# Block-sparse attention with a gated FFN: the first batch's k and q in fp32 on the hardware DMA queue, v loaded directly beside its ones column, weights held back, filler matmuls at the head

## The chip, the cores and the metric

The kernel runs on one core of one Trainium2 chip. The metric is the device time of one execution in microseconds (us). The kernel before took 298.56 us (median; 298.49 to 298.87). A profile gives the span from the first to the last instruction, which is just under 2 us shorter than the device time of the same run. The profiled run is a run of its own: that of the kernel before took 299.34 us.

Engine names follow the profile: PE is the matmul engine, PEld its weight load, DVE the vector engine, ACT the scalar engine, POOL the GpSimd engine, SP the engine that issues part of the DMAs. "L272" is line 272 of the kernel in question, so the same statement has different numbers in different kernels.

## The reference, cut to what matters

```python
def _attn_ref(q, k, v, sampled_blocks):          # q, k, v: (4, 8, 768, 64) fp32
    scores = scale * np.matmul(q, k.transpose(0, 1, 3, 2))
    mask = ...   # blocks of 32: neighbours, first and last row and column, 3 sampled blocks
    scores = np.where(mask, scores, -1000000000.0)
    scores = scores - np.max(scores, axis=-1, keepdims=True)
    attn = np.exp(scores)
    attn = attn / (np.sum(attn, axis=-1, keepdims=True) + 1e-09)
    return np.matmul(attn, v)

def _moe_ref(x, w_gate, w_val, w_out):           # x: (3072, 512), from the attention's output
    gate = 1.0 / (1.0 + np.exp(-(x @ w_gate)))
    val = x @ w_val                              # 512 -> 1536
    return gate * val @ w_out                    # 1536 -> 512
```

## The kernel before: the parts that the change touches

The work is split into 12 units: 4 batches, and 3 query ranges of 256 tokens in each. A unit has 4 head pairs. The row sum of the softmax comes free: the tile `vex` holds v in columns 0 to 63 of every row and a constant 1.0 in column 64, so the product with the exponentials gives the sum as its 65th column. A small scheduler (`plan`) fixes, in Python, the order in which every engine gets its instructions. On the chip each engine then works through its list in that order.

Loads:

```python
    k16 = sing.tile([128, H, NT, D], f16)
    v16 = sing.tile([128, H, NT, D], f16)
    vex = [sing.tile([128, H, NT, D + 1], f16, name=f"vex{r}") for r in range(2)]
    # ... cut ...
    def load_heads(dst, src, b, h0, h1, t0=0, t1=NT):
        nc.gpsimd.dma_start(                       # fp32 in DRAM, cast to f16 by the DMA
            dst[:, h0:h1, t0:t1, :],
            src[b, h0:h1].rearrange("h (p t) d -> p h t d", t=NT)[:, :, t0:t1, :],
        )
    # ... cut ...
    nc.sync.dma_start(e64, e64_h.ap())
    nc.scalar.dma_start(sbi, sampled_blocks)
    nc.sync.dma_start(mc, mc_h.ap())
    nc.sync.dma_start(ident, ident_h.ap())
    for p in range(NP):
        load_heads(k16, k, 0, 2 * p, 2 * p + 2)
        load_heads(q16, q, 0, 2 * p, 2 * p + 2, 0, 2)      # only unit 0's part of q
        load_heads(v16, v, 0, 2 * p, 2 * p + 2)
    load_w(0)
    load_heads(q16, q, 0, 0, H, 2, NT)                     # the rest of q: units 1 and 2
    for j in range(1, NF // FCH):
        load_w(j)
    # ... cut ...
    nc.vector.memset(mb16, 0.0)
    junk = sing.tile([128, 512], f16)
    nc.vector.memset(junk, 0.0)
    for r in range(2):
        nc.vector.memset(vex[r][:, :, :, D : D + 1], 1.0)  # the ones column
```

The head of the program: the block mask is made on DVE, one matmul with the constant `e` spreads it into `bias`, and v is copied into `vex` by DVE:

```python
    def mask_blocks(eng):
        sbf = sing.tile([NB, 3], f32, name="sbf")
        nc.vector.tensor_copy(sbf, sbi.bitcast(u16)[:, 0:12:4])
        nc.vector.tensor_tensor(mc[:, :, 1:4], ...)        # cut: is_equal
        # ... cut: tensor_reduce into mb16 ...

    warm(6)                                                # 6 matmuls on zeros
    t_mb = plan.add([(DVE, 0.7)], mask_blocks, at=2.5)
    # ... cut ...
    mm = plan.add([(PE, 0.25)], bias_mm, [t_mb], take=[bank])        # reads e and mb16
    plan.add([(PE, 0.9)], lambda eng: warm(2), [mm])

    def vcopy(b, p, deps, at):
        def go(eng):
            nc.vector.tensor_copy(
                vex[b % 2][:, 2 * p : 2 * p + 2, :, 0:D],
                v16[:, 2 * p : 2 * p + 2, :, :],
            )
        # ... cut ...
```

Each pair's k and q go through a DVE copy (`pr`), PE transposes, and a copy into `kT` and `qT`. From batch 1 on, DMA transposes issued by SP do this instead. Batch 1's own loads, all with `load_heads`, are:

```python
            def load(eng):
                for dst, src in ((k16, k), (q16, q), (v16, v)):
                    load_heads(dst, src, 1, 0, H)
```

The softmax here doesn't subtract the row's maximum and nothing guards it: scores larger than these inputs give would overflow.

## Time and profile before

| | kernel before |
|---|---|
| device time, median (range) | 298.56 us (298.49 to 298.87) |
| span of the profiled run | 297.6 us |
| PE busy | 289.9 us, 97% |
| first q·k matmul of unit 0 / 1 / 2 / 3 | 7.61 / 25.45 / 42.81 / 65.67 us |
| every later unit | 22.64 us after the one before |

Profile page of the kernel before: busy us, share of the span and instructions; then the busy share of PE, and the granted clock, in 40 equal slices as tenths (9 is 90% or more); then the chain of waits by engine.

```profile
PE 289.9 (97%) x3302; PEld 206.2 (69%) x3302; DVE 191.0 (64%) x439; ACT 205.1 (69%) x323; POOL 48.5 (16%) x65
...
PE   7998999999999999999999999999999999999994
...
PEclk9999999999999999999999999999999999999999
...
PE 92%; ACT 2%; DMA 2%; DVE 1%; POOL 1%; issue 0%; ACTq 0%; POOLq 0%
```

PE is full in every slice but the first ones. A change of the loads can only win in the head.

Timeline of PE in the kernel before: start, duration, engine, line, operation, output and input; in brackets the idle time before it and what ended it.

```profile
4.19 0.60 PE L300 MATMUL m<-e,mb 24*128 24x512 f16 x1 [0.20 <-DVE mb L252]
...
9.64 1.03 PE L382 MATMUL m<-ident,pr 128*128 128x128 f16 x8 [0.37 <-DVE pr L373]
10.61 0.39 PE L451 MATMUL s<-bias,e 64*128 64x256 f16 x2
10.80 0.42 PE L459 MATMUL s<-qT,kT 64*128 64x256 f16 x2
...
14.27 0.27 PE L459 MATMUL s<-qT,kT 64*128 64x256 f16 x2
14.38 0.27 PE L451 MATMUL s<-bias,e 64*128 64x256 f16 x2
...
15.46 0.61 PE L382 MATMUL m<-ident,pr 128*128 128x128 f16 x8
```

The same eight transposes take 1.03 us at 9.64 and 0.61 us at 15.46: PE runs at half rate at first. The page's clock row says 9 throughout and does not show this. The trace's clock records fit it: there is none before 13.30 us, and that one says full rate.

The chain of waits of the kernel before, in order of time: start, duration, what.

```profile
2.78 0.70 POOL v L188
3.48 5.72 DMA k<-in_k_dram
9.20 0.02 issue
9.23 0.37 DVE pr L373
9.60 0.05 issue
9.64 1.03 PE m L382 x8
```

The second pair's k holds PE until 9.64 us. This wait and the half rate are what the change aims at.

### The profile page before, as it was taken

The page shows a single profiled execution, that of the slowest core. Times are in us where ns is not written, and L with a number is a line of the kernel's source. Part 1 is how long each engine was busy: PE and PEld are TensorE (multiplying, and loading weights), DVE is VectorE, ACT ScalarE, POOL GpSimd, SP SyncE. Part 2 cuts the span into 40 slices and gives each one's busy share as a digit, 9 for nine tenths or more (in the row PEclk, how much of TensorE's full clock was granted, in tenths as well). Part 3 has the DMA queues.
Part 4 walks back from the last instruction along what each step waited for, and adds up shares of the span by engine and source line. Part 5 has one row for each costly group of instructions (what it writes and reads, how often), then busy time and mean ns, then how long its engine had stood idle before and what let it go on. Part 6 is the DMA issues. An engine that isn't in the chain of part 4 may idle for free.

```text
span 297.6 us, 7862 instructions
## 1 busy us (share of the span) xinstructions
PE 289.9 (97%) x3302; PEld 206.2 (69%) x3302; DVE 191.0 (64%) x439; ACT 205.1 (69%) x323; POOL 48.5 (16%) x65
## 2 busy tenths in 40 slices
PE   7998999999999999999999999999999999999994
PEld 2655785786786786786776786686687687687771
DVE  3588877875675677676576577577477477475240
ACT  2689977677677677677777776777777677672331
POOL 8944100197000000097100000000000000000000
PEclk9999999999999999999999999999999999999999
DMA  7999999999900200999940202920201200201101
GB/s 109 185 201 203 206 204 205 212 174 149 193 12 9 90 13 10 173 177 133 179 70 18 83 11 56 203 64 20 79 11 20 79 11 20 78 15 20 70 2 71
DMA packets 74540, 28.55 MB, mean 96 GB/s; under 512 B 57352, under 2 KB 71560, under 8 KB 74504
## 3 DMA queue, kind: packets, MB, share of 16 engines
q0 software_dynamic: 40400, 14.16, 43.7%
q1 hardware_dynamic: 33924, 13.75, 20.5%
q8 instruction: 26, 0.43, 0.6%
q10 hardware_dynamic: 180, 0.13, 0.1%
q14 instruction: 10, 0.08, 0.1%
HBM read 28.55 MB, written 6.29 MB: 117 GB/s over the span
## 4 chain that ended last, share of the span: by engine, by line
PE 92%; ACT 2%; DMA 2%; DVE 1%; POOL 1%; issue 0%; ACTq 0%; POOLq 0%
PE m L617 44%; PE m L657 22%; PE s L459 12%; PE m L497 12%; DMA k<-in_k_dram 2%; ACT pt L469 2%; PE s L451 1%; PE m L382 1%; PE m L347 1%; ACT qT L232 0%; PE m L518 0%; POOL k L188 0%; ACT kT L232 0%; POOL q L188 0%; POOL v L188 0%
## 5 line engine op out<-in xcount | busy, mean ns | idle before, releaser
L469 ACT ACTIVATE pt<-s 128x1024 f16<-128x1024 f32 x144 | 139.9, 1023 | 9.5 <-PE s L459 9.4
L475 DVE TENSOR_TENSOR pt<-pt,mask 128x1024 f16<-128x1024 f16 x132 | 91.0, 690 | 52.0 <-ACT pt L469 51.9
L628 ACT ACTIVATE th<-m 128x256 f32<-128x256 f32 x144 | 54.3, 388 | 48.0 <-PE m L617 47.2
L617 PE MATMUL m<-xT,wg 128*128 128x256 f16 x576 | 86.8, 273 | 0.3 <-DVE x L509 0.3
L617 PE MATMUL m<-xT,wv 128*128 128x256 f16 x576 | 86.4, 273 | 0.0
L633 DVE SCALAR_TENSOR_TENSOR ht<-th,m 128x256 f16<-128x256 f32 x144 | 56.6, 417 | 20.8 <-ACT th L628 20.5
L657 PE MATMUL m<-wo,ht 128*128 128x512 f16 x288 | 66.1, 380 | 0.0
L617 PEld LDWEIGHTS <-wv 128*128 128x128 f16 x576 | 56.3, 98 | 6.5
L617 PEld LDWEIGHTS <-wg 128*128 128x128 f16 x576 | 50.5, 98 | 14.8 <-issue 9.7
L657 PEld LDWEIGHTS <-ht 128*128 128x128 f16 x288 | 26.5, 98 | 32.8 <-issue 4.2
L459 PE MATMUL s<-qT,kT 64*128 64x256 f16 x576 | 48.0, 275 | 1.1 <-ACT pt L469 0.8
L497 PEld LDWEIGHTS <-pt 128*128 128x128 f16 x1152 | 43.3, 98 | 3.8 <-issue 0.6
L497 PE MATMUL m<-vex,pt 128*128 128x65 f16 x1152 | 45.1, 194 | 0.0
L459 PEld LDWEIGHTS <-kT 64*128 64x128 f16 x576 | 23.0, 95 | 17.4 <-issue 13.6
L694 ACT ACTIVATE ysb<-m 128x512 f32<-128x512 f32 x23 | 13.7, 597 | 23.7 <-PE m L657 23.7
L740 POOL DMA_DIRECT2D kp<-in_k_dram x16 | 13.0, 820 | 80.8 <-DMA kT<-kp 53.7
L509 DVE TENSOR_TENSOR x<-m,rz 128x256 f16<-128x256 f32 x48 | 20.4, 424 | 1.7
L507 DVE RECIPROCAL rz<-m 128x4 f32<-128x4 f32 x48 | 8.7, 181 | 15.1 <-PE m L497 15.1
L740 POOL DMA_DIRECT2D qp<-in_q_dram x16 | 13.0, 819 | 2.2 <-DMA kp<-in_k_dram 1.9
L451 PE MATMUL s<-bias,e 64*128 64x256 f16 x48 | 7.2, 319 | 0.2 <-ACT pt L469 0.2
L382 PE MATMUL m<-ident,pr 128*128 128x128 f16 x48 | 5.2, 264 | 0.8 <-DVE pr L373 0.4
L234 DVE CAST mask<-m 128x512 f16<-128x512 f32 x9 | 5.7, 681 | 0.4 <-PE m L347 0.4
(45 smaller groups left out, 67.2 us busy)
## 6 DMA issues: line engine op xcount, KB each, us to landing
out_dram<-ysb SPq DMA_DIRECT2D x23, 256.0 KB, 2.0
v<-in_v_dram POOLq DMA_DIRECT2D x3, 768.0 KB, 11.1
wg<-in_moe_w_gate_dram POOLq DMA_DIRECT2D x4, 384.0 KB, 12.8
wv<-in_moe_w_val_dram POOLq DMA_DIRECT2D x4, 384.0 KB, 14.0
wo<-in_moe_w_out_dram POOLq DMA_DIRECT2D x3, 512.0 KB, 16.9
kp<-in_k_dram POOLq DMA_DIRECT2D x16, 96.0 KB, 5.8
qp<-in_q_dram POOLq DMA_DIRECT2D x16, 96.0 KB, 4.9
k<-in_k_dram POOLq DMA_DIRECT2D x4, 192.0 KB, 5.8
```

The lines of the kernel that those rows point to most:

```text
L451: nc.tensor.matmul(score[self.bank.slot][:, o // D, i, :], e64[o : o + D, t * 128 : (t + 1) * 128], bias[o : o + D, :], start=True, stop=F ...
L459: nc.tensor.matmul(score[self.bank.slot][:, o // D, i, :], kT[b % 2][o : o + D, p, t * 128 : (t + 1) * 128], qT[b % 2][o : o + D, p, u * U ...
L469: nc.scalar.activation(self.pt, score[self.bank.slot], AF.Exp, bias=0.0, scale=SCALE)
L475: nc.vector.tensor_tensor(self.pt, self.pt, m.unsqueeze(1).broadcast_to([128, 2, 2, UQ]), op=ALU.mult,)
L497: nc.tensor.matmul(self.acc[:, s, a, :], self.steps[t // 2].pt[:, a, t % 2, s * 128 : (s + 1) * 128], vex[self.b % 2][:, 2 * self.p + a, t ...
L509: nc.vector.tensor_tensor(self.x16, self.acc[:, :, :, 0:D], rz.broadcast_to([128, 2, 2, D]), op=ALU.mult,)
L617: nc.tensor.matmul(pg[:, i, :], w[:, c, f * 128 : (f + 1) * 128], xTs[self.n][0][:, c, :], start=(c == 0), stop=(c == 3),)
L628: nc.scalar.activation(th, spare[bank.slot][:, 0:UQ], AF.Tanh, bias=0.0, scale=0.5)
L633: nc.vector.scalar_tensor_tensor(self.ht[:, f, :], in0=box[0], scalar=1.0, in1=spare[bank.slot][:, UQ : 2 * UQ], op0=ALU.add, op1=ALU.mult,)
L657: nc.tensor.matmul(spare[bank.slot], self.ht[:, f, s * 128 : (s + 1) * 128], wo[:, f, :], start=(f == 0), stop=(f == NF - 1),)
L694: nc.scalar.activation(ysb, spare[bank.slot], AF.Copy, bias=0.0, scale=0.5)
L740: nc.gpsimd.dma_start(dst[:, p, :, a, :], src[b, 2 * p + a].rearrange("(n t) d -> n t d", t=NT),)
```

## The change

The intent has four parts.

- The first batch's k and q come in fp32 through the SP queue. The DVE copies, which exist anyway, cast them.
- v is cast by its load and lands directly in columns 0 to 63 of `vex`, one DMA per head. The 16 DVE copies of v fall away, in all batches.
- The rest of q and the weights are held back until the second pair's k has been copied.
- 14 small matmuls on zeros fill PE's early gaps, so that the clock is released sooner.

```diff
+    k32 = (twice...)                    # cut: k of batch 0 in fp32 shares its tile with k16 and kp
+    q32 = sing.tile([128, H, UQ // 128, D], f32)
-    v16 = sing.tile([128, H, NT, D], f16)
+    def load_values(b, h0, h1):
+        for h in range(h0, h1):
+            load_heads(vex[b % 2][:, :, :, 0:D], v, b, h, h + 1)
-    nc.sync.dma_start(e64, e64_h.ap())
     nc.scalar.dma_start(sbi, sampled_blocks)
-    nc.sync.dma_start(mc, mc_h.ap())
-    nc.sync.dma_start(ident, ident_h.ap())
+    nc.scalar.dma_start(mc, mc_h.ap())
     for p in range(NP):
-        load_heads(k16, k, 0, 2 * p, 2 * p + 2)
-        load_heads(q16, q, 0, 2 * p, 2 * p + 2, 0, 2)
-        load_heads(v16, v, 0, 2 * p, 2 * p + 2)
-    load_w(0)
-    load_heads(q16, q, 0, 0, H, 2, NT)
-    # cut: the other weights
+        load_heads(k32, k, 0, 2 * p, 2 * p + 2, eng=nc.sync)
+        load_heads(q32, q, 0, 2 * p, 2 * p + 2, 0, 2, eng=nc.sync)
+        if p == 0:
+            nc.sync.dma_start(ident, ident_h.ap())
+            nc.sync.dma_start(e64, e64_h.ap())
+        load_values(0, 2 * p, 2 * p + 2)
+    def load_rest(gate):                 # called at the second pair's copy of k
+        first = load_heads(q16, q, 0, 0, H, 2, NT)
+        tc.add_manual_dep(first.ins, gate.name, ...)          # cut
+        # cut: all weights
@@ the ones column stays where it was, now after these loads in the program @@
     for r in range(2):
         nc.vector.memset(vex[r][:, :, :, D : D + 1], 1.0)
@@
+    for _ in range(FILL):                # FILL = 14
+        filler()                         # a 128x256 matmul on zeros, when nothing else is ready
-    plan.add([(PE, 0.9)], lambda eng: warm(2), [mm])
-    # cut: vcopy and its calls
@@ batch 1 @@
-                for dst, src in ((k16, k), (q16, q), (v16, v)):
+                for dst, src in ((k16, k), (q16, q)):
                     load_heads(dst, src, 1, 0, H)
+                load_values(1, 0, H)
@@ cut: batches 2 and 3 load v with load_values too; costs and landing times in the scheduler @@
```

More of the change, by code (lines that the diff above doesn't have):

```diff
@@ L37 @@
 FFN_LAG = 3
+GATE = 1
+FILL = 14
 TOK = (np.arange(S) % 128) * NT + np.arange(S) // 128
@@ L64, in __init__, with add @@
         self.tasks = []
+        self.rank = []
         self.room = {kind: [(0.0, i) for i in range(n)] for kind, n in banks.items()}
-    def add(self, engines, fn, deps=(), at=0.0, take=(), free=(), lag=None):
+    def add(self, engines, fn, deps=(), at=0.0, take=(), free=(), lag=None, late=0):
         self.tasks.append((engines, fn, list(deps), at, list(take), list(free), lag))
+        self.rank.append(len(self.tasks) - 1 + late)
         return len(self.tasks) - 1
@@ L77, in run @@
                 after[d].append(i)
-        ready = sorted(i for i in range(n) if not left[i])
+        ready = sorted((i for i in range(n) if not left[i]), key=self.rank.__getitem__)
         busy = {PE: 0.0, ACT: 0.0, DVE: 0.0, DMA: 0.0}
@@ L90, in run @@
                     if not left[j]:
-                        bisect.insort(ready, j)
+                        bisect.insort(ready, j, key=self.rank.__getitem__)
             if events and events[0][0] <= now:
@@ L177 @@
     q16 = sing.tile([128, H, NT, D], f16)
-    k16 = sing.tile([128, H, NT, D], f16)
     qp = sing.tile([128, NP, NT, 2, D], f16, name="qp")
-    kp = sing.tile([128, NP, NT, 2, D], f16, name="kp")
-    v16 = sing.tile([128, H, NT, D], f16)
+    twice = sing.tile([128, 2, H * NT * D], f16, name="twice")
+    k16 = twice[:, 0, :].rearrange("a (h t d) -> a h t d", h=H, t=NT)
+    kp = twice[:, 1, :].rearrange("a (p t h d) -> a p t h d", p=NP, t=NT, h=2)
+    k32 = (
+        twice.rearrange("a r n -> a (r n)")
+        .bitcast(f32)
+        .rearrange("a (h t d) -> a h t d", h=H, t=NT)
+    )
+    q32 = sing.tile([128, H, UQ // 128, D], f32)
     vex = [sing.tile([128, H, NT, D + 1], f16, name=f"vex{r}") for r in range(2)]
@@ L184, with load_heads @@
     kT = [sing.tile([128, NP, S], f16, name=f"kT{r}") for r in range(2)]
-    def load_heads(dst, src, b, h0, h1, t0=0, t1=NT):
-        nc.gpsimd.dma_start(
+    def load_heads(dst, src, b, h0, h1, t0=0, t1=NT, eng=None):
+        return (eng or nc.gpsimd).dma_start(
             dst[:, h0:h1, t0:t1, :],
@@ L196, in load_w @@
         f0, f1 = j * FCH * 128, (j + 1) * FCH * 128
-        for dst, src in ((wg, moe_w_gate), (wv, moe_w_val)):
+        return [
             nc.gpsimd.dma_start(
@@ L200, in load_w @@
             )
+            for dst, src in ((wg, moe_w_gate), (wv, moe_w_val))
+        ][0]
     def load_wo(j):
@@ L209 @@
     sbi = sing.tile([NB, 3], mybir.dt.int64)
-    nc.sync.dma_start(e64, e64_h.ap())
     nc.scalar.dma_start(sbi, sampled_blocks)
-    nc.sync.dma_start(mc, mc_h.ap())
-    nc.sync.dma_start(ident, ident_h.ap())
+    nc.scalar.dma_start(mc, mc_h.ap())
     for p in range(NP):
-        load_heads(k16, k, 0, 2 * p, 2 * p + 2)
-        load_heads(q16, q, 0, 2 * p, 2 * p + 2, 0, 2)
-        load_heads(v16, v, 0, 2 * p, 2 * p + 2)
-    load_w(0)
-    load_heads(q16, q, 0, 0, H, 2, NT)
-    for j in range(1, NF // FCH):
-        load_w(j)
-    for j in range(3):
-        load_wo(j)
+        load_heads(k32, k, 0, 2 * p, 2 * p + 2, eng=nc.sync)
[6 more added lines that the diff above has]
+        first = load_heads(q16, q, 0, 0, H, 2, NT)
+        tc.add_manual_dep(
+            first.ins,
+            gate.name,
+            mybir.DependencyInfo(
+                mybir.DependencyClass.Sync, mybir.DependencyReason.DATA
+            ),
+            reason="k, q and v of batch 0 come first",
+        )
+        for j in range(NF // FCH):
+            load_w(j)
+        for j in range(3):
+            load_wo(j)
     mb16 = sing.tile([NB, 128], f16)
@@ L270, in m16 @@
         return spare[slot].bitcast(f16)
-    landed = 3.9
+    landed = 2.6
     land = {}
     for p in range(NP):
-        for nm, mb in (("k", 0.393), ("q", 0.131), ("v", 0.393)):
+        for nm, mb in (("k", 0.393), ("q", 0.131), ("v", 0.393 if p else 0.6)):
             landed += mb / DMA_RATE
             land[nm, p] = landed
-    for nm, mb in (("w", 0), ("q2", None), ("w", 1), ("w", 2), ("w", 3)):
+    for nm, mb in (("q2", None), ("w", 0), ("w", 1), ("w", 2), ("w", 3)):
         landed += (1.05 if mb is None else 1.573) / DMA_RATE
@@ L293, with filler, go @@
     warm(6)
+    def filler():
+        bank = Bank("m")
+        def go(eng):
+            nc.tensor.matmul(
+                spare[bank.slot][:, 0:UQ], junk[:, 0:128], junk[:, 0:UQ], start=True, stop=True
+            )
+        plan.add([(PE, 0.22)], go, at=3.0, take=[bank], free=[bank], late=5000)
+    for _ in range(FILL):
+        filler()
     t_mb = plan.add([(DVE, 0.7)], mask_blocks, at=2.5)
@@ L372, in pair @@
             box.append(pr)
-            nc.vector.tensor_copy(
+            ins = nc.vector.tensor_copy(
                 pr[:, t0:t1, :, :],
@@ L378, in pair @@
             )
+            if src is k32 and p == GATE:
+                load_rest(ins.ins)
         def turn(eng):
@@ L395, in prep @@
         n = t1 - t0
-        a = plan.add([(DVE, 0.15 + 0.035 * n)], pair, ring("pr", PB) + loaded[b], at=at)
+        cost = 0.13 + (0.07 if t0 == 0 else 0.035) * n
+        a = plan.add([(DVE, cost)], pair, ring("pr", PB) + loaded[b], at=at)
         copies[b].append(a)
@@ L424, in xbar, with load_v @@
         return plan.add([(DMA, 0.01)], go, deps, lag=10.0)
-    def vcopy(b, p, deps, at):
+    def load_v(b, deps, at=0.0, lag=20.0):
         def go(eng):
-            nc.vector.tensor_copy(
-                vex[b % 2][:, 2 * p : 2 * p + 2, :, 0:D],
-                v16[:, 2 * p : 2 * p + 2, :, :],
-            )
-        a = plan.add([(DVE, 0.36)], go, loaded[b] + deps, at=at)
-        copies[b].append(a)
-        return a
+            load_values(b, 0, H)
+        return plan.add([(DMA, 0.01)], go, deps, at=at, lag=lag)
     class Step:
@@ L534, in value @@
                 lambda eng: self.pv(0),
-                self.products + [vdone[self.b, self.p]],
+                self.products + vdone[self.b, self.p],
                 take=[self.bank],
@@ L726, in prep_k, with prep_v @@
     def prep_k(b, p, at=0.0):
-        kdone[b, p] = [prep(k16, kT, b, p, 0, NT, [], at)]
+        kdone[b, p] = [prep(k32, kT, b, p, 0, NT, [], at)]
     def prep_q(b, p, at=0.0, t0=0, t1=NT):
-        d_ = [prep(q16, qT, b, p, t0, t1, [], at)]
+        d_ = [prep(q16 if t0 else q32, qT, b, p, t0, t1, [], at)]
         for u in range(t0 // 2, t1 // 2):
             qdone[b, p, u] = d_
-    def prep_v(b, p, at=0.0):
-        vdone[b, p] = vcopy(b, p, read.get(("pv", b - 2, p), []), at)
+    def prep_v(b):
+        done = load_v(b, [x for p in range(NP) for x in read.get(("pv", b - 2, p), [])])
+        for p in range(NP):
+            vdone[b, p] = [done]
     def pair_load(dst, src, b):
@@ L778, in load @@
                 pair_load(qp, q, b)
-                load_heads(v16, v, b, 0, H)
             ld = plan.add(
@@ L793, in later @@
                     qdone[b, p, u] = [turned_b["q", b]]
-        for p in range(0, NP, 2):
-            at = land["v", "next"] if b == 1 else 0.0
-            preps.append(lambda p=p, at=at: [prep_v(b, p + i, at) for i in range(2)])
+        if b == 1:
+            t_v = plan.add([(DMA, 0.01)], lambda eng: None, loaded[1], at=land["v", "next"], lag=0.0)
+            for p in range(NP):
+                vdone[1, p] = [t_v]
+        else:
+            preps.append(lambda: prep_v(b))
     def do(queue, fn):
@@ L810 @@
         prep_q(0, p, land["q", p], 0, 2)
-        prep_v(0, p, land["v", p])
+        t_v = plan.add([(DMA, 0.01)], lambda eng: None, at=land["v", p], lag=0.0)
+        vdone[0, p] = [t_v]
     for p in range(NP):
```

## The prediction

> **What bounds it now.** PE is busy 97% of the 297.6 us span (engine table), and 10.00 of every 10 us from 40 us on (windows table): PE work that this change does not touch. Only the head can give. In the timeline:
> - Up to 5.9 us PE does only junk matmuls and one mask matmul. First transposes 5.90, first q·k 7.60, first exp 8.47.
> - Second pair: the chain of waits names the k load, 3.48 to 9.20 us; transposes start at 9.64.
> - PE runs at half rate until about 13.4 us: q·k matmuls are 0.21 us apart at 9–13 us, 0.11 us from 14 us; eight transposes take 1.03 us at 9.64, 0.61 us at 15.46. The granted clock reads 1.00 throughout and does not show this. The Trainium skill ("TensorE: Matmul & The Clock Gate", Part 1) says PE starts at half clock and is released after about 3.4 us of sustained work; this trace agrees: 13.4 is 3.8 us after the last PE gap (9.28–9.64).
> - From 13.4 to 25 us the chain is PE, then ACT (qT copies, exps) to 29 us; ACT is 9.28 busy of 10 us in 20–30.
>
> **What changes.**
> - k and q go by the SP queue in fp32. The constant e load (192 KB, rows as long as k's) landed at 285–300 GB/s in its best half microsecond; the Pool queue at about 150 GB/s (of half-size output) up to 9 us. Estimate: k0 lands 3.8–4.0 instead of 5.4, k1 near 7 instead of 9.2, k2 9.5, k3 12.
> - e and ident now queue behind k0 and q0 (750 KB up to e's end): e lands near 5.2–5.5 (before, 3.1). The bias matmul needs e and PE is in order, so transposes, with three fillers before them, start near 6.3 and the first q·k near 7.9: 0.3 us lost, although k0 is early.
> - Fillers close the PE gaps from about 5.4 us, so the full rate should come at 9–12 us instead of 13.4. The main gain: 1 to 2 us on a chain that is PE there. They cost 14×0.11–0.21 us of mostly idle PE.
> - The second pair no longer waits for DMA; once PE is full, about 0.3 us.
> - DVE loses 16 v copies of 0.36 us; 8 casts get dearer by an estimated 0.1–0.25 us. Under 0.3 us on the chain.
> - The rest of q lands near 14 instead of 22 us, which removes part of the 24–26 us chain (qT copies, 1.1 us). Weights wait for the second pair's copy but total bytes are the same: first gate weights land near 19 us, needed at about 27; wo needed near 45. No loss expected.
> - v in 128-byte rows: later k/q loads of that form ran at 150 GB/s against 200, off the chain.
>
> **Sum.** −0.3 (first q·k) +1.7 (rate) +0.3 +0.2 +0.7 = about 2.6 us, all before 35 us, carried to the end. Predicted 296.0 us, eight in ten between 294.0 and 298.2. Chances: faster by over 2% 0.04, within 2% 0.95, slower 0.01.
>
> **What would show it.** Right: q·k spacing falls to 0.11 us at 9–12 us; first k cast near 4 us but bias matmul at 5–5.5; first exp 8–9; first FFN matmul (29.28 before) 2–3 us earlier; from there to the end unchanged within 0.5 us. Wrong: bias matmul by 4.3 and first exp near 7 (gain 4 us or more); full rate only at 13 us (under 1 us); PE waits on weights around 27–45.
>
> **What would make it wrong.** The shared DMA engines may starve k or v (first pair's v after 9 us would stall its products); releasing the clock may need less continuous work than thought; after 25 us ACT may hold everything; the new PE order may open gaps later.

## More of the kernel before

Timeline of DVE in the kernel before: start, duration, engine, line, operation, output and input; in brackets the idle time before it and what ended it.

```profile
0.92 0.27 DVE L238 MEMSET junk<- 128x256 uint32 x1
1.32 0.31 DVE L240 MEMSET vex<- 128x48 f16 x2
2.99 0.16 DVE L244 CAST sbf<-sbi 24x3 f32<-24x3 uint16 x1 [1.36 <-DMA sbi<-in_sampled_blocks_dram]
```

The ones column is written from 1.32 us on, and the mask's first instruction runs at 2.99 us, as soon as its small load has landed.

## The result, and the profile after

The kernel after took 312.69 us (median of four runs, 312.13 to 313.98) against 298.56 us. The ratio is 1.0477, with a 95% interval of 1.0444 to 1.051: slower. Ratios here are the mean time of one kernel's runs over that of the other's runs of the same rounds, so they are not quite the ratio of the quoted medians. Executions over 1.5% slower than the fastest of the same kernel are left out of the means. All runs gave correct results.

First q·k matmul of each unit (us):

| unit | before | after | difference |
|---|---|---|---|
| 0 | 7.61 | 22.94 | +15.33 |
| 1 | 25.45 | 38.86 | +13.41 |
| 2 | 42.81 | 56.69 | +13.88 |
| 3 | 65.67 | 80.28 | +14.61 |
| 11 | 246.80 | 261.41 | +14.61 |

The whole loss is there before the first q·k matmul, and the spans differ by the same 14.6 us (312.2 against 297.6).

Profile page of the kernel after, same rows.

```profile
PE 290.5 (93%) x3314; PEld 206.4 (66%) x3314; DVE 188.3 (60%) x426; ACT 203.4 (65%) x320; POOL 63.1 (20%) x82
...
PE   4049999999999999999999999999999999999995
...
PEclk9559999999999999999999999999999999999999
...
PE 86%; DMA 7%; POOL 2%; ACT 1%; DVE 1%; issue 1%; DVEq 0%; ACTq 0%; POOLq 0%
```

PE does the same work (290.5 us) but stands still in the second slice, and the granted clock falls to half there.

Timeline of DVE in the kernel after.

```profile
0.92 0.27 DVE L266 MEMSET junk<- 128x256 uint32 x1
18.50 0.37 DVE L272 CAST sbf<-sbi 24x3 f32<-24x3 uint16 x1 [17.30 <-DMA vex<-in_v_dram]
18.56 0.31 DVE L268 MEMSET vex<- 128x48 f16 x2
```

Timeline of PE in the kernel after.

```profile
3.79 0.63 PE L327 MATMUL m<-junk 128*128 128x256 f16 x2
19.64 0.60 PE L341 MATMUL m<-e,mb 24*128 24x512 f16 x1 [15.22 <-DVE mb L280]
```

The chain of waits of the kernel after.

```profile
4.63 2.42 POOL vex L199 x3
7.05 11.18 DMA vex<-in_v_dram
18.23 0.03 issue
18.26 0.05 DVEq L268
18.31 0.14 issue
...
18.50 0.41 DVE sbf L272
18.93 0.23 DVE mc L273
```

DVE does nothing from 1.2 to 18.5 us. The profile attaches the wait of 17.30 us to the cast of the sampled blocks (L272), which reads nothing of v. The chain shows who really waited: DVE's sequencer at L268, the memset of the ones column. It waits for the loads of v into the other columns of the same tile. The lists of the two compiled programs say it plainly. DVE's list before, then after, with the semaphores that each instruction waits for:

```
before   3 L240 Memset vex_79 128x48
         4 L240 Memset vex_80 128x48
         5 L244 TensorCopy sbf<-sbi 24x3 [waits DMAHW3_49]
after    3 L268 Memset vex_78 128x48 [waits DMASW4_49,DMASW5_49,DMASW3_49,DMASW6_49,DMASW2_49,DMASW7_49,DMASW1_49,DMASW0_49]
         4 L268 Memset vex_79 128x48
         5 L272 TensorCopy sbf<-sbi 24x3 [waits DMAHW2_49]
```

In the kernel before, nothing had written `vex` ahead of the memset. Now eight loads stand ahead of it in the program, and the memset of that tile waits for all eight, although the bytes are disjoint. This wait is part of the program: it was put there when the kernel was built. The memset of the other `vex` tile has no wait. Everything behind the memset on DVE stands still too: the mask, the casts of k and q, and so the transposes on PE. The Trainium skill ("TensorE: Matmul & The Clock Gate", Part 1, "Architectural detail") says that ACT's and DVE's queues are strict FIFO. This trace agrees: the cast at L272 could start at 2.99 us in the kernel before and started at 18.50 us here.

### The profile page after: what moved, and what is told of

Same layout as the page of the kernel before. It is cut to its first block, busy times and chain, and to the rows that moved or that the text cites. A ratio compares the mean times of both kernels' runs of the same rounds, so it can differ in the third digit from the quotient of the medians.

```text
span 312.2 us, 7920 instructions
## 1 busy us (share of the span) xinstructions
PE 290.5 (93%) x3314; PEld 206.4 (66%) x3314; DVE 188.3 (60%) x426; ACT 203.4 (65%) x320; POOL 63.1 (20%) x82
## 3 DMA queue, kind: packets, MB, share of 16 engines
q1 hardware_dynamic: 36064, 15.84, 22.2%
## 4 chain that ended last, share of the span: by engine, by line
PE 86%; DMA 7%; POOL 2%; ACT 1%; DVE 1%; issue 1%; DVEq 0%; ACTq 0%; POOLq 0%
PE m L655 38%; PE m L695 21%; PE s L497 12%; PE m L535 11%; DMA qT<-qp 4%; DMA vex<-in_v_dram 4%; POOL vex L199 2%; PE s L489 1%; PE m L424 1%; ACT pt L507 1%; PE m L327 1%; PE m L387 1%; DVE pt L513 0%; PE m L556 0%; ACT th L666 0%
## 5 line engine op out<-in xcount | busy, mean ns | idle before, releaser
L507 ACT ACTIVATE pt<-s 128x1024 f16<-128x1024 f32 x144 | 140.2, 1023 | 10.2 <-PE s L497 10.0
L199 POOL DMA_DIRECT2D vex<-in_v_dram x32 | 26.2, 823 | 15.2 <-DMA wo<-in_moe_w_out_dram 5.2
L780 POOL DMA_DIRECT2D twice<-in_k_dram x16 | 13.0, 819 | 55.4 <-DMA kT<-twice 55.4
L260 ACT COPY kT<-m 128x768 f16<-128x768 f16 x1 | 0.8, 798 | 19.7 <-PE m L424 19.7
## 6 DMA issues: line engine op xcount, KB each, us to landing
wv<-in_moe_w_val_dram POOLq DMA_DIRECT2D x4, 384.0 KB, 12.6
```

Source lines behind the costliest of these rows:

```text
L199: return (eng or nc.gpsimd).dma_start(dst[:, h0:h1, t0:t1, :], src[b, h0:h1].rearrange("h (p t) d -> p h t d", t=NT)[:, :, t0:t1, :],)
L507: nc.scalar.activation(self.pt, score[self.bank.slot], AF.Exp, bias=0.0, scale=SCALE)
L780: nc.gpsimd.dma_start(dst[:, p, :, a, :], src[b, 2 * p + a].rearrange("(n t) d -> n t d", t=NT),)
```

## The experiments

Each ratio is against the kernel before in the same rounds. The medians of the kernel before in the four sets of runs were 298.57, 298.83, 298.85 and 298.66 us. The runs of a set share a chip and their rounds; ratios of different sets are compared with more caution.

### Set 1: is it the order of the memset, and is that all?

The main theory (A) was that the memset's wait alone costs the time. The rivals were that the loads themselves come late, because narrow rows of v and fp32 k and q share the DMA engines (B), and that holding the weights back is what costs (C).

**ones_first** is the kernel after with the memsets moved ahead of all loads:

```diff
+    mb16 = sing.tile([NB, 128], f16)
+    nc.vector.memset(mb16, 0.0)
+    junk = sing.tile([128, 512], f16)
+    nc.vector.memset(junk, 0.0)
+    for r in range(2):
+        nc.vector.memset(vex[r][:, :, :, D : D + 1], 1.0)
     mc = sing.tile([NB, NB, 4], f32)       # ... the loads follow; the same lines below are removed
```

> The changed kernel with one thing moved: the memset of the ones column stands ahead of the v loads in the program instead of after them, so that it waits for no load. Theory A (that memset waits for all eight v loads, 17.3 us, and holds everything on DVE behind it): the first mask cast on DVE is back near 3 us, and the whole loss goes: 294 to 298 us, about 16 us under the changed kernel. Rival B (the loads themselves come late, because v in 128-byte rows and k and q in fp32 share the DMA engines; the wait only shows it): the DVE waits move to the k casts or the products wait for v, and the time stays over 305 us. Rival C (holding the weights back is what costs): their release at the second k cast comes early again, so C alone is not told apart here.

Measured: ratio 1.0128 (1.0096 to 1.0161), runs of 300.97 to 303.81 us; a sixth run, slow, took 305.64. The cast of the sampled blocks no longer waits for v (DVE timeline of ones_first):

```profile
2.99 0.47 DVE L272 CAST sbf<-sbi 24x3 f32<-24x3 uint16 x1 [1.36 <-DMA sbi<-in_sampled_blocks_dram]
```

The first q·k matmul moved from 22.94 back to 9.00 us. So the order accounts for the difference of the ratios, 3.5% or about 10.4 us of the 14.2 us loss; the profiled spans (312.2 and 302.0) differ by 10.2. But the repaired kernel is still slower than the kernel before, where the prediction, and the expectation of 294 to 298 us for this run, had a gain.

**before_v** takes the kernel before and adds only the direct loads of v, with the memset after them:

```diff
-        load_heads(v16, v, 0, 2 * p, 2 * p + 2)
+        load_values(0, 2 * p, 2 * p + 2)
     # likewise in batches 1 to 3; vcopy removed; nothing else of the change
```

> The kernel before with only the v part of the change: v loaded straight beside the ones column, memset after the loads, as the change has it. No fp32 loads, no hold on the weights, no fillers. A: the memset waits until the last of the v loads, which are spread among k and q on the Pool queue, at 15 to 18 us; 308 to 314 us. B and C: the DMA mix and the hold are not there, so within 3 us of 298.6.

Measured: 312.08 us, ratio 1.0456 (1.0437 to 1.0476). The one part reproduces nearly the whole loss (1.0456 of 1.0477), without fp32 loads, fillers or held weights. Waits of this kernel: engine, line, what for; us in total, times, longest.

```profile
DVE sbf L247 <- DMA vex<-in_v_dram: 16.3, 1, 16.3
```

**before_v_ones** is the same kernel with the memsets first:

```diff
+    for r in range(2):                     # with the memsets of mb16 and junk before it
+        nc.vector.memset(vex[r][:, :, :, D : D + 1], 1.0)
     mc = sing.tile([NB, NB, 4], f32)       # ... the loads follow
```

> The same with the memset ahead of the loads. A: the loss is gone, 296 to 301 us; what is left against 298.6 is the price of 16 instead of 12 load issues on the Pool queue at the head (0.7 to 0.8 us each; k of the second pair lands about 0.8 us later) less 16 v copies of 0.36 us on DVE. B: no different from before_v.

Measured: 303.03 us, ratio 1.0144 (1.0127 to 1.016). The wait of 16.3 us is gone, and 9 us with it; 296 to 301 us was expected, so more is left than theory A had. The 1.4% that remain are the price of v's direct loads alone, since nothing else of the change is in this kernel. Here, where k, q and v all share the Pool queue, the loss arises in the head: the fourth pair's transposes wait 1.66 us for k at 16.98 us, the clock records show half rate from 19.07 to 22.48 us, and unit 1 starts at 28.96 instead of 25.45 us. At 69.25 us PE waits another 0.88 us for batch 1's transposed q, and unit 3 starts 3.58 us later than in the kernel before.

**ones_nofill** is ones_first without fillers:

```diff
-FILL = 14
+FILL = 0
```

> ones_first without the 14 filler matmuls. If the fillers do what they were put in for (close the gaps so that PE comes to full rate sooner), PE reaches 0.11 us per q-k matmul 1 to 4 us later than in ones_first and the time is 0.5 to 2 us longer. If the fillers only stand in front of real work, the time is 0.3 to 1 us shorter.

Measured: 304.78 us, ratio 1.0203 (1.0173 to 1.0233). So the timed runs take 0.75% or about 2.2 us longer without fillers, and the fillers are not the cause of the second loss. The first lasting record of full rate is at 11.15 us with them and at 13.37 us without. But the profiles do not show that the sooner rate earns the 2.2 us. Without fillers, units 1 and 2 start sooner (24.66 and 42.19 us, against 25.05 and 42.89), and the profiled run is no slower (303.23 us, against 303.81). What the kernel without fillers has of its own is a wait for the transposed q of batch 2, far from the head:

```profile
137.46 0.61 PE L497 MATMUL s<-qT,kT 64*128 64x256 f16 x8 [2.20 <-DMA qT<-qp]
```

Its instruction lists differ too: PE has 88 instead of 84 matmuls with each of `wg` and `wv` before unit 3. The number came out near the expectation, and its mechanism is not shown.

The windows tables of ones_first show a detour on the way to full rate. Columns: window in us and its length; busy us (instructions) of PE, PEld, DVE, ACT, POOL; granted clock; DMA share; GB/s. ones_first:

```profile
4.40:7.60 3.20, 1.27 (x12) 0.78 (x11) 1.99 (x6) 0.13 (x1) 3.20 (x5) 1.00 1.26 219
7.80:11.10 3.30, 3.13 (x23) 1.67 (x24) 1.05 (x3) 1.67 (x3) 1.93 (x3) 0.50 1.58 249
11.20:14.20 3.00, 3.00 (x55) 2.20 (x53) 1.92 (x6) 2.54 (x3) 0.96 (x2) 1.00 1.72 224
```

The clock was already released at 4.32 us. PE was busy only 1.27 of the 3.20 us from 4.40 us on, above all because the mask's matmul waited for `e`. The clock then fell back for one period of 3.41 us.

Waits of ones_first:

```profile
PE m L341 <- DMA e<-bb_e: 1.9, 1, 1.9
```

Where did the second loss of ones_first arise? Its units 1 and 2 start as before (25.05 and 42.89 against 25.45 and 42.81 us), and unit 3 at 68.57 against 65.67. In the kernel before, PE did not wait there:

```profile
65.67 0.61 PE L459 MATMUL s<-qT,kT 64*128 64x256 f16 x8
```

Timeline of PE in ones_first:

```profile
65.22 0.60 PE L655 MATMUL m<-xT,wv 128*128 128x256 f16 x4
68.57 0.61 PE L497 MATMUL s<-qT,kT 64*128 64x256 f16 x8 [2.75 <-DMA qT<-qp]
69.12 1.02 PE L655 MATMUL m<-xT,wg 128*128 128x256 f16 x4
```

PE waits 2.75 us for batch 1's transposed q. Right after it, four matmuls of the same size take 1.02 instead of 0.60 us: the clock records show half rate from 69.17 to 72.59 us, one period of 3.41 us. Unit 4 starts at 92.79 us, 4.47 later than in the kernel before (88.32). That is the whole of the second loss in this profile, whose span is 4.4 us longer. Two of the timed runs, at a mean clock of 1.000, took only 301 us.

Why is qT late? The transposing DMA of q took longer and was issued later. DMA issues between 46 and 72 us in the kernel before; the last number is us from issue to landing.

```profile
qT<-qp SPq DMA_TRANSPOSE x1, 7.1
```

The same of ones_first.

```profile
qT<-qp SPq DMA_TRANSPOSE x1, 10.1
```

SP's timeline has the issue at 55.05 us in the kernel before and at 58.31 us in ones_first, after a kT transposition that took SP 7.85 instead of 6.17 us. Meanwhile the eight loads of batch 1's v are still coming. In ones_first POOL issues the last three of them at 43.85, 47.70 and 51.60 us, each after a wait for an earlier DMA, and they take 10.6 to 12.6 us to land. In the kernel before, v of batch 1 was a single load, issued at 30.54 us. Windows of the kernel before, columns as above:

```profile
52.00:55.00 3.00, 3.00 (x42) 1.88 (x41) 2.11 (x6) 1.68 (x3) 0.00 (x0) 1.00 1.26 200
55.00:58.00 3.00, 3.00 (x46) 2.78 (x45) 2.74 (x9) 2.32 (x4) 0.00 (x0) 1.00 1.22 200
```

The same windows of ones_first.

```profile
52.00:55.00 3.00, 3.00 (x41) 1.86 (x40) 2.31 (x6) 1.58 (x3) 0.42 (x1) 1.00 2.03 144
55.00:58.00 3.00, 3.00 (x47) 2.77 (x46) 2.01 (x6) 2.32 (x4) 0.00 (x0) 1.00 1.48 136
```

The DMA share is above 1.00 in both, so on average each engine has more than one packet under way, but they move 136 to 144 instead of 200 GB/s. The Trainium skill ("DMA: Bandwidth & Descriptors", Specifications) says that line rate needs at least 512 bytes and that below it the engine does a read-modify-write. The v loads write rows of 128 bytes (64 halves beside the ones column) where the loads into `v16` wrote runs of 768 bytes. In 14.0 to 15.0 us, where casting loads alone run in both, ones_first moved 152 GB/s in packets of 128 bytes and the kernel before 202 in packets of 768. That the engine reads before it writes, no run here shows.

### Set 2: does the order of batch 1's loads matter, and the hold on the weights?

If the tail of v only collides with the transposes because v comes last, then v first should mend it (theory D). The rival (E) was that holding the weights back made all loads of batch 1 late.

**v1_first** is ones_first with v first in batch 1:

```diff
             def load(eng):
+                load_values(1, 0, H)
                 for dst, src in ((k16, k), (q16, q)):
                     load_heads(dst, src, 1, 0, H)
-                load_values(1, 0, H)
```

> ones_first with one more thing moved: for batch 1 the eight narrow-row v loads are issued ahead of its k and q instead of behind them. In ones_first PE had no work from 65.8 to 68.4 us, waiting for the q transpose of batch 1, and then ran 3.4 us at half clock; while k and q were transposed (49 to 68 us) the Pool queue was still bringing v in 128-byte rows up to 60 us. Theory D (that tail of v takes the DMA engines from the transposes): the transposes run after v has landed, qT lands by 64, no PE gap, no drop of the clock; 4.4 us saved, 297.5 to 300 us. Rival E (holding the weights made all loads of batch 1 late): nothing changes, 302 to 304 us.

Measured: 303.39 us, ratio 1.0146 (1.0125 to 1.0168). A miss for D; the time is the one that E had. k and q now landed later instead (q at 57.25 us), DVE waited 4.7 us for k, and the mask multiplications behind that wait on DVE held PE in three short gaps. Unit 3 started at 69.48 us. The wait moved and did not shrink.

**v1_nohold** is v1_first without the added dependency that holds back the rest of q and the weights:

```diff
-        tc.add_manual_dep(first.ins, gate.name, ...)
```

> v1_first without the hold on the weights: the rest of q and the weights are issued right behind the v loads. The hold cost the Pool queue only 1.4 us of waiting in ones_first. Theory D: within 1 us of v1_first. Theory E: faster than v1_first by 1.5 to 4 us.

Measured: 302.86 us, ratio 1.0124 (1.0101 to 1.0147). This is not distinguishable from v1_first: the hold is worth nothing that these rounds can show, and E, which had 1.5 to 4 us, falls too. What remained was that v's loads cost their time wherever they stand.

**v1_e** is v1_first with `e` ahead of k and q on the SP queue, and `ident` on ACT's:

```diff
+    nc.sync.dma_start(e64, e64_h.ap())
     nc.scalar.dma_start(sbi, sampled_blocks)
     nc.scalar.dma_start(mc, mc_h.ap())
+    nc.scalar.dma_start(ident, ident_h.ap())
     # the lines for e64 and ident after the first pair are removed
```

> v1_first, with the constant e ahead of k on the SP queue and ident on the ACT queue. In ones_first the bias matmul waited for e until 6.29 us, PE stood still from 4.4 us and the clock fell back at 7.74. If e's place behind k and q is what ate the head's gain: the bias matmul comes at 4.7 to 5.2 us, the first q-k matmul 1 to 1.5 us earlier than in v1_first, and the time is 1 to 2.5 us under it, 295.5 to 298 us. If not, it is within 0.5 us of v1_first.

Measured: 303.45 us, ratio 1.0142 (1.0105 to 1.0178). A miss: this is within 0.5 us of v1_first, where 295.5 to 298 was expected. The first q·k matmul came at 8.08 us (v1_first 9.84), but unit 1 started at 27.14 us: PE waited 1.86 us for the rest of q at 21.14 us and fell back to half rate from 22.80 to 26.22 us. The early gain was given back.

**v1_e_nofill** is v1_e without fillers:

```diff
-FILL = 14
+FILL = 0
```

> v1_e without the 14 fillers. In ones_nofill the clock came to full at 13.4 us, in ones_first at 11.15 for good. If the fillers bring the clock up sooner: this is 0.5 to 2 us slower than v1_e and its clock record shows full rate later. If they only delay work: same or faster.

Measured: 305.61 us, ratio 1.0215 (1.019 to 1.0239). Without fillers the kernel takes 0.73% or about 2.2 us longer here too, as in set 1. Again the profile does not put this in the head: units 0 to 2 start 0.6 to 0.8 us sooner without fillers, and PE then waits 1.31 us for the mask's multiplication at 58.76 us and 1.81 and 1.88 us for the transposed q of batches 1 and 2 (71.32 and 140.31 us). v1_e has only waits of 0.36 and 0.56 us in their place.

### Set 3: wide rows for the later batches, and parts of the change alone

**ones_later_wide** is ones_first with v of batches 1 to 3 loaded as in the kernel before. Only batch 0 is loaded directly. The rival (E2) was that the part for batch 0 alone makes everything behind it late:

```diff
+    v16 = sing.tile([128, H, NT, D], f16)           # and vcopy, as before
             def load(eng):
-                for dst, src in ((k16, k), (q16, q)):
+                for dst, src in ((k16, k), (q16, q), (v16, v)):
                     load_heads(dst, src, 1, 0, H)
-                load_values(1, 0, H)
```

> ones_first with v of batches 1 to 3 loaded as the kernel before does (wide rows into a staging tile, DVE copies beside the ones column); only batch 0 keeps the direct narrow-row v load. Putting v ahead of k and q (v1_first) only made k and q late instead (q landed at 56.9, unit 3 began at 69.48 against 65.67 before), so the order is not the point; what is left of theory D is that v in narrow rows costs DMA time wherever it stands. If so: qT of batch 1 lands by 64.5, unit 3 starts at 65.7 to 66.3, total 298 to 299.8 us. Rival E2 (the batch-0 part, with fp32 k and q and narrow v, has already put the weights and everything behind them 1.5 to 2 us late, and that alone is over the slack): unit 3 still starts at 67 or later, 301 us or more.

Measured: 300.5 us, ratio 1.0046 (1.0021 to 1.0072), against 1.0128 for ones_first. The wait for qT is gone. PE timeline of this kernel:

```profile
65.23 0.60 PE L667 MATMUL m<-xT,wv 128*128 128x256 f16 x4
65.76 0.61 PE L509 MATMUL s<-qT,kT 64*128 64x256 f16 x8
66.30 0.61 PE L667 MATMUL m<-xT,wg 128*128 128x256 f16 x4
```

DMA issues of this kernel between 46 and 72 us:

```profile
qT<-qp SPq DMA_TRANSPOSE x1, 7.4
```

So the direct loads of v in the later batches are the second cause, by way of batch 1's transposes, and they are worth 0.8% or about 2.4 us. That is the difference of one change within the code, but of two sets of runs. The profiled span is 297.7 us against 297.6 of the kernel before; the timed runs are 0.46% slower, a little more than expected, and the profiled one is among the fastest. The rest of the change thus gains nothing.

**kq_hw** undoes the direct loads of v in all batches and keeps fp32 k and q on the SP queue, the hold and the fillers, with `e` first:

```diff
-        load_values(0, 2 * p, 2 * p + 2)
+        load_heads(v16, v, 0, 2 * p, 2 * p + 2)      # and vcopy in every batch, as before
```

> All v loads wide with DVE copies, as before; the rest of the change kept: k and q of the first batch in fp32 by the SP queue, with e ahead of k and ident on the ACT queue, weights held, fillers. No narrow rows and no memset problem. If narrow rows are the whole of what is left: the head is 1 to 3 us faster (unit 2 at 40 to 42 against 42.81) and unit 3 starts at 64 to 65.7: 295.5 to 298.5 us. Under E2: 299 to 302 us.

Measured: 302.04 us, ratio 1.0088 (1.0052 to 1.0124), with a wide spread (299.47 to 303.14). Another miss: 295.5 to 298.5 was expected if narrow rows were all that was left. Without narrow rows anywhere the kernel is still no faster. In its profile the third k cast waits for its load until 14.04 us (11.56 in the kernel before), and there is a stretch at half rate from 32.68 to 36.09 us after a stretch in which PE waited for ACT. later_wide_e of set 4 differs from this kernel only by the direct loads of v in batch 0, and is no slower (1.0016). For batch 0 the direct loads of v are therefore not what hurts in this order of loads.

**before_fill** adds only the fillers to the kernel before, in place of its two matmuls on zeros after the mask's matmul:

```diff
+    for _ in range(FILL):
+        filler()
-    plan.add([(PE, 0.9)], lambda eng: warm(2), [mm])
```

> The kernel before with only the 14 fillers (and without its two junk matmuls behind the bias matmul, as in the change). If fillers bring the clock up sooner: full rate before 11.5 us instead of 13.3, unit 2 starts 0.5 to 2 us sooner, 296.5 to 298.2 us. If they only stand before real work: 298.5 to 299.5 us.

Measured: 300.47 us, ratio 1.0054 (1.0023 to 1.0085), another miss. Full rate came at 6.80 instead of 13.30 us. Unit 3 did not come earlier: 65.73 against 65.67 us, and the span is 297.6 us in both profiles. The rate released 6.5 us sooner bought nothing, and the windows tables show where it went. Up to 65.67 us both kernels have run the same matmuls, but for 12 more on zeros here (734 and 746). PE stood idle 3.86 us in the kernel before and 5.13 here, and its matmuls on zeros took 3.78 and 5.82 us. Together that is 3.3 us more, which is what the full rate took off the other matmuls. The longest waits are for the second and third pairs' copies of k (0.61 us at 9.64 us and 1.17 us at 11.98 us), whose loads land no sooner than in the kernel before (the third at 11.54 against 11.53 us). The unprofiled runs are slower than the profiled one, and the slowest has the lowest mean clock: 302.86 us at 0.989, 300.16 to 301.04 us at 0.994, 299.45 us at 0.999. That fits a clock that falls back in gaps, but a timed run without a profile doesn't show where.

### Set 4: what holds the head

By then it was open why a head with earlier loads and an earlier full rate did not start unit 3 sooner. The candidate was the rest of q, which in the kernel before lands at 22.2 us, behind the first weights (G; H stands for its being something else).

**before_q** takes the kernel before and only moves the rest of q ahead of the first weights:

```diff
-    load_w(0)
     load_heads(q16, q, 0, 0, H, 2, NT)
-    for j in range(1, NF // FCH):
+    for j in range(NF // FCH):
         load_w(j)
     # and the same order in the scheduler's table of landing times
```

> The kernel before with only the rest of q moved ahead of the first weights. Under both, no gain or little: PE at half rate until 13.3 us is what holds unit 1 there, as q was waited for by nobody in the profile of before; 298 to 299.5 us, unit 3 at 65.2 to 65.9.

Measured: 298.26 us (297.8 to 298.39), ratio 0.9981 (0.9968 to 0.9995). It is the only version with a ratio below 1, by 0.2% or about 0.6 us. The rest of q is copied from 18.73 us on, and unit 3 starts at 64.55 us. In the profiled run the clock also happened to be released at 4.96 us, so the profile mixes two effects; the ratio over five rounds does not rest on that one run.

**fill_q** is before_q with before_fill's fillers (edit against the kernel before; the loop over the other weights is cut):

```diff
+    for _ in range(FILL):
+        filler()
-    plan.add([(PE, 0.9)], lambda eng: warm(2), [mm])
-    load_w(0)
     load_heads(q16, q, 0, 0, H, 2, NT)
```

> before_fill with the rest of q issued ahead of the first weights (and the plan told so). G: no wait for q near 22 us, unit 3 starts 0.8 to 2.5 us sooner than 65.7, 296 to 299 us where before_fill had 300.5. H: unit 3 within 0.3 us of 65.7.

Measured: 300.86 us, ratio 1.0062 (1.0034 to 1.009). Unit 3 started at 66.04 us. If the load of q alone had held the head, fillers and early q together should have gained; they did not. PE waited 1.50 us, until 11.86 us, for the copy of the third pair's k, whose load landed at 11.41 us, and 1.09 us, until 19.36 us, for DVE's scaling of the first output.

**later_wide_e** is ones_later_wide with `e` first, as in v1_e. It is the change with every defect repaired that was found:

```diff
+    nc.sync.dma_start(e64, e64_h.ap())
     nc.scalar.dma_start(sbi, sampled_blocks)
     nc.scalar.dma_start(mc, mc_h.ap())
+    nc.scalar.dma_start(ident, ident_h.ap())
```

> ones_later_wide with e ahead of k on the SP queue and ident on the ACT queue. The bias matmul comes about 1.2 us sooner and PE is at full rate by 9 to 10 us, but in v1_e the rest of q, behind the narrow v of batch 0, was waited for until 20.8 us. G: that wait comes again and unit 3 starts at 65.4 to 66.5, 299 to 301 us. H: the same.

Measured: 299.43 us, ratio 1.0016 (1.0 to 1.0032). Against ones_later_wide the order of `e` makes 0.3% or 0.9 us, but the two intervals overlap and come from different sets, so this is not shown. What is left of the change is a kernel as fast as the one before, not a faster one. PE waits 1.32 us at 20.78 us for the copy of the rest of q, and 0.26 us for ACT at 29.04 us.

### The sum

| step, from after back to before | ratio | worth |
|---|---|---|
| after | 1.0477 | |
| memsets ahead of the loads (ones_first) | 1.0128 | 3.5%, 10.4 us |
| later batches' v in wide rows (ones_later_wide) | 1.0046 | 0.8%, 2.4 us |
| `e` ahead of k and q (later_wide_e) | 1.0016 | 0.3%, 0.9 us |
| what is left | 1.0 | 0.2%, 0.5 us |

The third column is the difference of the ratios times 298.6 us. The rows come from four different sets and each ratio has an interval of 0.2 to 0.3% to either side, so only the first two steps are well separated from nothing. The second cause cost the kernel after itself only 0.7 us: with everything 15 us later its loads were nearly done in time (PE waited 0.7 us for qT). It came to light when the first was repaired.

## Why the prediction was wrong

The prediction said 296.0 us (294.0 to 298.2). The kernel took 312.69.

- **The step that failed: "bias matmul at 5–5.5".** It took for granted that DVE's head stays as it was and that only the loads of k, q and `e` set that time. The prediction costed what DVE loses (16 copies of v) and what gets dearer (8 casts), but not the order of what stays. The memset of the ones column, 0.31 us of work, stood behind eight new loads of its own tile. It waited for them until 18.3 us and held DVE's whole queue. The bias matmul ran at 19.64 us. before_v shows this with that part alone (ratio 1.0456), and ones_first shows it by undoing the order alone.
- **"v in 128-byte rows … off the chain" was wrong as well.** The rate was about right (152 against 202 GB/s). The place was wrong: the tail of batch 1's v shared the DMA engines with the transposes of batch 1's k and q, and qT came 2.75 us too late for PE, which then ran at half rate for 3.41 us. ones_later_wide removes it.
- **"e lands near 5.2–5.5" was too early.** With the memsets first, `e` landed at 6.25 us, 4.0 us after its issue (2.4 in the kernel before), and the first q·k came at 9.00, not 7.9 us. The Trainium skill ("DMA: Bandwidth & Descriptors", "Issuing engines are not separate DMA queues") says that all DMAs end up on the same 16 engines and interleave. This trace agrees: v's loads by POOL start at 1.73 us and run beside k, q and `e`.
- **"k1 near 7, k2 9.5" was too early.** k0 did land at about 4.0 us as predicted. But k1 landed at 8.2 us (9.2 before) and k2 at 11.4 us (11.5 before). That sharing the engines with v is the reason is argued, not shown by a run of its own; narrow rows are not needed for it, since in kq_hw, with v in wide rows, k1 and k2 landed later still (10.46 and 14.02 us). The same page ("Issuing engine by pattern") calls the hardware queues generally faster. Here the move to SP, with fp32 rows and another order of loads, was worth 1.0 us and 0.2 us in all.
- **"The rest of q lands near 14" was wrong.** It landed at 19.8 us in ones_first, against 22.2 before. It was issued at 9.77 us, behind v's loads on the Pool queue, and took 10.0 us.
- **"The main gain: 1 to 2 us" of the fillers: the rate came as predicted, its worth did not.** Full rate came for good at 11.15 us in ones_first (predicted 9 to 12). The timed kernels without fillers are 2.2 us slower, but in the profiles they are ahead in the head, and the waits that they have of their own lie at batches 1 and 2. So the nearness of 2.2 to the predicted 1.7 us is luck as far as the record shows. In the kernel before, full rate 6.5 us sooner gave nothing at unit 3, since PE spent what it won on matmuls on zeros and on waits; there the fillers cost 0.5%.
- **The sum failed for a second reason:** gains at different points of the head were added up and "carried to the end". Unit 3 starts at 65.76 and 66.06 us with the repairs, and at 65.67 before. ACT is busy 9.28 of 10 us between 20 and 30 us in the kernel before. That PE's earlier start ends in waits for DVE's copies of k and for ACT is seen in the traces; that ACT is the floor of the head is argued and not shown.

What stays open: whether the narrow rows of v or the larger number of DMAs (eight instead of one in batch 1) does more of the harm, which no run separates; which resource sets the floor of the head; why the kernels without fillers wait for the transposed q of batch 2; and why timed runs of the versions with fillers scatter more (299.45 to 302.86 us for before_fill against 298.44 to 299.85 us for the kernel before in the same rounds).

## What to carry to other kernels

When a load is moved into part of a tile, look at every other writer of that tile in program order, because a constant that was written first for free may now wait behind the load, and on an in-order engine everything behind it waits too. When a profile shows a long wait on an instruction that has no use for the thing it waits for, look at the instruction just ahead of it. Gains in the head of a program should be counted at the first point where the old and the new kernel do the same work (here unit 3), and many narrow loads are not free where a transfer that is waited for shares the engines at that time.

## What the Trainium skill lacked or had wrong

- No page says that a memset of one column of a tile can be ordered behind DMA loads into other columns of the same tile. "TensorE: Matmul & The Clock Gate" has the FIFO that makes it costly; the runs show 17.3 us of DVE standing still in the kernel after, and 16.3 us in before_v.
- "TensorE: Matmul & The Clock Gate", Part 1: its free-running window of about 3.4 us agrees (every short stretch at one rate in these traces lasts 3.41 us or a multiple of it). Its idle rule ("HAM oscillation": no idle gaps above about 3.4 us) is too mild here. In ones_first PE had 1.27 us of work spread over 3.20 us, with no gap above 1.87 us, and still lost its clock, and a gap of 2.75 us at 65.8 us was followed by one period at half rate too. These traces give no share of busy time as the limit: before_q kept its clock through a period with 1.78 of 3.41 us busy and ones_later_wide lost it after one with the same 1.78 us; ones_nofill kept it through one with 1.42, and kq_hw lost it after one with 2.37.
- The same page warns in general that clock events in a trace can be unreliable, but has no word on records that begin late: the granted clock of the kernel before reads full from the start, while the first record comes at 13.30 us and eight transposes take 1.03 us before it and 0.61 us after it.
- "DMA: Bandwidth & Descriptors", Specifications: it gives the limit of 512 bytes but no size of the loss; its "Why small descriptors are slow" has a cost per packet (27% at 256 bytes), but nothing measured for narrow loads that cast. Casting loads with rows of 128 bytes ran at 152 GB/s where runs of 768 bytes ran at 202; with DMA transposes beside them, all DMAs together moved 136 to 144 GB/s.
- "DMA: Bandwidth & Descriptors" does not say what a load does to a DMA transpose beside it: the transpose of q took 10.1 us in ones_first, with narrow loads before and beside it, and 7.4 and 7.1 us without them.
